# Linformer attention followed by a hard-swish feed-forward: when one load of q starts, and one weight load cut in two

## The chip, the cores and the metric

The kernel runs on one core of a Trainium2 chip. A core has TensorE (PE, the matrix engine), VectorE (DVE), ScalarE (ACT), GpSimd (POOL) and SyncE (SP), each with its own instruction queue that runs in order. Transfers between HBM and the on-chip memory are issued from such a queue and carried out by 16 DMA engines. In this kernel POOL issues all loads (the profile's queue q0, software_dynamic) and SP all stores, DMA transposes and re-layouts but a few (q1, hardware_dynamic). The metric is the device time of one execution in microseconds.

## The reference

```
def _attn_ref(q, k, v, E, F):                 # q, k, v: 8 batches, 8 heads, 1024 tokens, 64
    k_proj = einsum('ks,bhsd->bhkd', E, k)    # 1024 tokens projected to 64
    v_proj = einsum('ks,bhsd->bhkd', F, v)
    scores = matmul(q, k_proj^T) / sqrt(64)
    attn   = softmax(scores)                  # over the 64 projected keys
    return matmul(attn, v_proj)

x = attn_out as 8192 tokens x 512
h = x @ w_in                                  # 512 -> 2048
g = h * clip(h + 3, 0, 6) / 6
out = g @ w_out                               # 2048 -> 512, float32
```

## The kernel before

**Stages.** A batch has 1024 tokens, handled as two blocks of 512. For a block, the first product (`first_group`, one call for each of 16 groups of 128 columns of w_in) makes h in PSUM, 8 matmuls each; ACT and DVE turn it into g (`h_out`). The second product (`second_group`) multiplies g by w_out, in four parts of 128 tokens, each in four quarters over the 2048 columns. All matmuls are cut into two halves of 64 columns (`in_columns`, line 169).

**Attention of the next batches** is laid between these groups. `project` multiplies k and v by E and F, `turn` has SP transpose the projected keys (kT, line 212) and q (qT, line 157), `scores` (line 229) multiplies qT and kT, `exps` takes the exponential on ACT, `add_up` and `spread_sums` build the softmax sums on DVE, take reciprocals, write them to DRAM (`turned_rows`, line 287, two small transfers) and read them back spread over the partitions (`rec`, line 293, eight transfers: two for each of four pairs of heads `recs[0]` to `recs[3]`). `values` (line 250) multiplies the weights by the projected v, and `scaled` (line 262) multiplies that by the reciprocals into xT, the input of the first product of the next batch.

**Order.** The schedule is written by hand: the order in the program is the order on each engine. In the main loop `plan` maps (part of the second product, quarter) to a step of attention. While batch 1 is in its feed-forward (b = 1), batch 2 is projected, its sums end at (5, 2), its values for pairs 0 and 1 come at (6, 1), its products with the reciprocals at (6, 4), and pairs 2 and 3 at (7, 1). Then b = 2 starts with `TwoGroups(...).parts((0, 1, 2), (3,))`: the first two groups of w_in take pairs 0, 1 and 2 of xT (12 matmuls) and then pair 3. Within b = 2 batch 3 is projected at (0, 2) and its scores come at (1, 4). Batch 3's qT is not made in `turn`: a step at the end of b = 1 puts its two DMA transposes on SP's queue ahead of batch 3's kT.

**Loads.** At the start POOL issues, in this order: k and the first half of q of batch 0 in pairs of heads, v of batch 0, w_in in eight pieces (two of 128 columns, five of 256, the last of 512), the second half of batch 0's q, w_out in four quarters, and k, v, q of batch 1. POOL's loads go round eight semaphores, and a load waits until the load eight places before it has landed. Later batches are loaded by `turn`: POOL copies one element (`mark`) of the last DMA transpose, which makes it wait for that transpose, and then issues the three loads of the next batch. The order is k, v, q, but for batch 3, where it is q, k, v. The k, v and q tiles have two buffers each.

Of the kernel before, what the change touches and what calls it, by code (L numbers as in the profile page):

```python
# [9 lines left out]
bf16 = mybir.dt.bfloat16  # L10
# [5 lines left out]
def kernel(  # L16
# [11 lines left out]
    nc = tc.nc  # L28
# [27 lines left out]
    att = ctx.enter_context(tc.tile_pool(name="att", bufs=2))  # L56
# [36 lines left out]
    def raw_tile(name):  # L93
        return kqv_pool.tile([P, H, SO, D], bf16, tag=name, name=name)


    kqv = {0: {n: raw_tile(n) for n in ("k", "q", "v")}}
# [16 lines left out]
        load_pair("v", j)  # L114

    def load_kqv(b, order="qkv"):
        kqv[b] = {}
        for n in order:
            kqv[b][n] = raw_tile(n)
            nc.gpsimd.dma_start(out=kqv[b][n], in_=kqv_dram[n][b])  # L120
# [3 lines left out]
    def load_w_in(lo, n):  # L124
        nc.gpsimd.dma_start(out=w_in_sb[:, :, lo:lo + n], in_=w_in_v[:, :, lo:lo + n])

    for lo, n in ((0, 128), (128, 128), (256, 256), (512, 256), (768, 256),
                  (1024, 256), (1280, 256), (1536, 512)):
        load_w_in(lo, n)
    load_q0(1, slice(0, H))  # L130
    for i in range(SB):
        c = slice(i * FO // SB, (i + 1) * FO // SB)
        nc.gpsimd.dma_start(out=w_out_sb[:, c, :], in_=w_out_v[:, c, :])
    load_kqv(1, "kvq")


# [16 lines left out]
    def q_transposed(b):  # L153

        t = qT_pool.tile([P, KO, 2, TOK], bf16, tag="qT", name="qT")
        for i in range(2):
            nc.sync.dma_start_transpose(t[:, i * KO // 2:(i + 1) * KO // 2].rearrange("p j a (m n) -> p (j a m) n", n=P),
                                        kqv[b]["q"][:, i * H // 2:(i + 1) * H // 2].rearrange("p h s d -> p (h s d)"))
        return t
# [11 lines left out]
    def rec_tile():  # L171
        return att.tile([P, 2, TOK], f32, tag="rec", name="rec", bufs=4)
# [9 lines left out]

    later = []

    class Attention:
# [23 lines left out]
        def turn(self):  # L211
            nc.sync.dma_start_transpose(self.kT, self.kp.rearrange("p h a d -> p (h a d)"))
            last = self.kT[:1, 0, :1]
            if self.b != 3:
                qT_dma[self.b] = q_transposed(self.b)
                last = qT_dma[self.b][:1, 0, 0, :1]
            if self.b + 1 < B:
                mark = att.tile([1, 1], bf16, tag="mark", name="mark")
                nc.gpsimd.tensor_copy(mark, last)  # L219
                load_kqv(self.b + 1, "qkv" if self.b == 2 else "kvq")  # L220


        def scores(self, j, *allocs):
# [52 lines left out]
        def spread_sums(self):  # L276
            turned, other = [att.tile([P, KO * 32], f32, tag="turned", name="turned", bufs=2) for _ in range(2)]
            inv = att.tile([KP, KO * 32], f32, tag="inv", name="inv", bufs=1)
            nc.vector.transpose(turned, self.parts.rearrange("p j c -> p (j c)"))
            for t in range(NB):  # L280
                here, there = slice(t * KP, t * KP + 32), slice(t * KP + 32, (t + 1) * KP)
                nc.vector.tensor_copy(other[here], turned[there])
                nc.vector.tensor_add(inv[t * 32:(t + 1) * 32], turned[here], other[here])
            nc.vector.reciprocal(inv, inv)
            rows = dram.tile([NB, KO, 32, 32], f32, tag="turned_rows", name="turned_rows")
            for t in range(NB):
                nc.sync.dma_start(out=rows[t].rearrange("j c i -> c j i"),
                                  in_=inv[t * 32:(t + 1) * 32].rearrange("c (j i) -> c j i", j=KO))
            by_head = rows.rearrange("t j (a c) i -> j a t (c i)", a=2)
            self.recs = [rec_tile() for _ in range(KO)]  # L290
            for j in range(KO):
                for a in range(2):
                    nc.sync.dma_start(out=self.recs[j][a * D:(a + 1) * D],
                                      in_=by_head[j, a:a + 1].to_broadcast([D, NB, TOK]))

# [434 lines left out]
```

## Time and profile before

| | us |
|---|---|
| median of 4 runs | 502.46 |
| lowest and highest | 502.1 to 504.07 |
| the profiled execution | 502.1 |
| its span, first to last instruction | 500.3 |
| PE busy | 494.0 (99%) |
| DVE, ACT, POOL busy | 285.5, 239.7, 38.7 |
| software DMA queue (POOL's loads) | 29.36 MB, 37.6% of 16 engines' span |
| hardware DMA queue (SP's and ACT's) | 38.02 MB, 30.6% |

The DMA row of the page, in 40 slices of 12.5 us, shows where transfers crowd: the first eight slices are at nine tenths or nearly so, and later slices go up and down with the loads of each batch.

```profile
DMA  9999999897759799449950799309411261101112
```

A timeline row of the profile gives the start, the length, engine, line, operation, what it writes and reads, and in brackets how long the engine idled before it and what ended that. For a DMA the length is the time its issue holds the queue; a row of DMA issues ends with the size of each and the time from its issue to its landing. Sizes are those of the bf16 destination.

### The profile page before, as it was taken

Reading aid. Unit: us, or ns where it says so; the run is one execution under the profiler, and the core shown is the slowest. Engines: PE = TensorE matmul, PEld = TensorE weight load, DVE = VectorE, ACT = ScalarE, POOL = GpSimd, SP = SyncE. Lnnn points to the kernel's source line nnn. Section 1 sums busy time; section 2 is a strip of 40 time slices with the busy share of each in tenths; the row PEclk is TensorE's granted clock in tenths of the full one; section 3 lists DMA queues with packets and bytes.
Section 4 is the critical chain, followed back from the end, with each engine's and each line's share of the span. In section 5 each row is a group of like instructions: output and inputs, shape, how many; then the busy total and the mean of one; then the engine's idle time right before and its main releaser. Section 6 shows DMA issues by size and latency. Waiting matters only on the chain.

```text
span 500.3 us, 11177 instructions
## 1 busy us (share of the span) xinstructions
PE 494.0 (99%) x4802; PEld 256.2 (51%) x4802; DVE 285.5 (57%) x438; ACT 239.7 (48%) x414; POOL 38.7 (8%) x58
## 2 busy tenths in 40 slices
PE   8899999999999999999999999999999999999997
PEld 4454554555455555555555545555455555555554
DVE  3572836886659674666648654674755656334420
ACT  3656566665355345433563344643446344343431
POOL 8620020200020020002000020000000000000000
PEclk9999999999999999999999999999999999999999
DMA  9999999897759799449950799309411261101112
GB/s 166 197 204 208 187 173 233 151 213 174 178 94 222 173 198 216 104 118 226 213 111 22 182 190 222 75 25 232 115 43 44 60 176 45 43 22 43 44 43 84
DMA packets 83618, 68.43 MB, mean 137 GB/s; under 512 B 38256, under 2 KB 69232, under 8 KB 83568
## 3 DMA queue, kind: packets, MB, share of 16 engines
q0 software_dynamic: 32480, 29.36, 37.6%
q1 hardware_dynamic: 50864, 38.02, 30.6%
q8 instruction: 37, 0.61, 0.5%
q10 hardware_dynamic: 224, 0.33, 0.3%
q14 instruction: 13, 0.11, 0.1%
HBM read 71.83 MB, written 16.97 MB: 177 GB/s over the span
## 4 chain that ended last, share of the span: by engine, by line
PE 96%; DMA 2%; POOL 2%; issue 0%; ACT 0%; ACTq 0%; POOLq 0%
PE mm L169 89%; PE at L169 2%; DMA v<-in_v_dram 2%; PE mm L250 1%; PE at L229 1%; PE at L250 1%; PE mm L229 1%; POOL q L102 1%; POOL k L106 1%; POOL v L106 0%; PE at L425 0%; PE at L405 0%; PE at L391 0%; PE at L418 0%; POOL ident masks.py:199 0%
## 5 line engine op out<-in xcount | busy, mean ns | idle before, releaser
L514 DVE SCALAR_TENSOR_TENSOR g<-r,mm 128x512 bf16<-128x512 f32 x256 | 174.4, 687 | 143.1 <-ACT r L513 142.4
L169 PE MATMUL mm<-w_out_sb,g 128*64 128x512 bf16 (+2 forms) x2080 | 235.7, 376 | 0.0
L169 PE MATMUL mm<-xT,w_in_sb 128*64 128x512 bf16 x2048 | 231.1, 379 | 0.0
L513 ACT ACTIVATE r<-mm 128x512 f32<-128x512 f32 x256 | 152.7, 598 | 74.2 <-PE mm L169 73.2
L169 PEld LDWEIGHTS <-g 128*64 128x64 bf16 x2080 | 115.0, 110 | 106.5 <-issue 7.3
L169 PEld LDWEIGHTS <-w_in_sb 128*64 128x64 bf16 x2048 | 115.9, 110 | 104.7 <-issue 0.6
L548 ACT COPY o_sb<-mm 128x512 f32<-128x512 f32 x58 | 34.0, 586 | 150.0 <-PE mm L169 149.6
L270 DVE TRANSPOSE_TENSOR_REDUCE parts<-aT 128x32 f32<-128x1024 bf16 x24 | 28.8, 1227 | 0.0
L262 DVE TENSOR_TENSOR xT<-at,rec 128x512 bf16<-128x512 f32 x32 | 20.5, 683 | 8.7 <-ACT rec L181 5.8
L238 ACT ACTIVATE aT<-at 128x512 bf16<-128x512 f32 x38 | 20.7, 620 | 7.6 <-PE at L229 7.6
L262 DVE TENSOR_TENSOR xT<-mm,rec 128x512 bf16<-128x512 f32 x24 | 15.5, 686 | 7.3 <-PE mm L250 7.2
L219 POOL COPY mark<-qT 1x1 bf16<-1x1 bf16 x5 | 0.9, 178 | 202.0 <-DMA qT<-q 202.0
L205 DVE CAST kp<-at 64x512 bf16<-64x512 f32 x14 | 9.0, 678 | 11.2 <-PE at L169 11.2
L169 PE MATMUL at<-k,e_t 128*64 128x512 bf16 x56 | 13.2, 379 | 0.0
L169 PE MATMUL at<-v,f_t 128*64 128x512 bf16 x56 | 13.2, 379 | 0.0
L238 ACT ACTIVATE aT<-mm 128x512 bf16<-128x512 f32 x18 | 9.7, 603 | 7.1 <-PE mm L229 7.1
L208 DVE CAST vp<-at 64x512 bf16<-64x512 f32 x14 | 9.7, 694 | 0.4
L538 DVE COPY o_sb<-mm 128x384 f32<-128x384 f32 x1 | 0.6, 558 | 15.1 <-PE mm L169 15.1
L169 PEld LDWEIGHTS <-e_t 128*64 128x64 bf16 x56 | 6.2, 110 | 5.7
L89 PE MATMUL mm<-ones 128*128 128x512 bf16 x18 | 6.8, 504 | 1.5 <-DVE ones L82 1.5
L229 PEld LDWEIGHTS <-kT 64*64 64x64 bf16 x224 | 5.7, 106 | 4.4 <-issue 3.5
L503 DVE TENSOR_TENSOR xT<-at,rec 128x512 bf16<-128x512 f32 x4 | 2.5, 684 | 8.2 <-PE at L425 8.2
(68 smaller groups left out, 151.3 us busy)
## 6 DMA issues: line engine op xcount, KB each, us to landing
out_dram<-o_sb SPq DMA_DIRECT2D x63, 256.0 KB, 4.4
rec<-turned_rows SPq DMA_DIRECT2D x48, 256.0 KB, 6.7
k<-in_k_dram POOLq DMA_DIRECT2D x7, 1024.0 KB, 10.5
v<-in_v_dram POOLq DMA_DIRECT2D x7, 1024.0 KB, 15.6
q<-in_q_dram POOLq DMA_DIRECT2D x7, 1024.0 KB, 20.4
w_out_sb<-in_moe_w_out_dram POOLq DMA_DIRECT2D x4, 512.0 KB, 16.1
w_in_sb<-in_moe_w_in_dram POOLq DMA_DIRECT2D x5, 256.0 KB, 10.0
k<-in_k_dram POOLq DMA_DIRECT2D x4, 256.0 KB, 5.5
```

The costliest lines, as they stand in the source:

```text
L89: nc.tensor.matmul(ps, ones[:, :P], ones, start=True, stop=True)
L169: nc.tensor.matmul(ps[lo:lo + width], stationary[:, lo:lo + width], moving, **flags)
L205: nc.vector.tensor_copy(self.kp[:, :, a, :], self.ps[:KP].rearrange("p (h d) -> p h d", d=D))
L208: nc.vector.tensor_copy(self.vp[a * KP:(a + 1) * KP], self.ps[KP:].rearrange("p (h d) -> p h d", d=D))
L229: nc.tensor.matmul(tiles[r][t * KP:(t + 1) * KP, a * HT:(a + 1) * HT], self.kT[r * D:(r + 1) * D, 2 * j + a, :], qT[r * D:(r + 1) * D, j, ...
L238: when(lambda r=r: nc.scalar.activation(aT[:, :, r, :], tiles[r].rearrange("p (a n) -> p a n", a=2), AF.Exp, scale=scale))
L250: nc.tensor.matmul(tiles[t][c:c + D], stationary(r, 2 * j + a), self.weights(j, a)[r:r + KP], start=True, stop=True)
L262: when(lambda t=t: nc.vector.tensor_mul(self.xT[:, j, t, :], av[t], rec[:, t]))
L270: nc.vector.tensor_reduce(out=self.parts[:, j], op=ALU.add, axis=mybir.AxisListType.X, apply_transpose=True, in_=self.aT[j].rearrange("p a ...
L513: nc.scalar.activation(r, h_ps, AF.Relu, bias=0.5, scale=1.0 / 6.0)
L514: nc.vector.scalar_tensor_tensor(g[:, fo, :], r, 1.0, h_ps, op0=ALU.min, op1=ALU.mult)
L548: (copy or nc.scalar.copy)(o_sb, o_ps)
```

## The change

`load_kqv` may now be called more than once for a batch. The mark and the load behind it have become a function, `behind_that`. For batch 3 `turn` of batch 2 now loads only k and v behind batch 2's qT. The load of batch 3's q is issued at the end of `spread_sums` of batch 2, behind a copy of one element of `recs[1]`, the third of the eight transfers that bring the reciprocals back. On POOL the copy stands behind the two loads and ahead of the mark for batch 4. The last 512 columns of w_in come in two loads of 256. No engine but POOL has another instruction or another order.

```
-        kqv[b] = {}
+        kqv.setdefault(b, {})
...
     for lo, n in ((0, 128), (128, 128), (256, 256), (512, 256), (768, 256),
-                  (1024, 256), (1280, 256), (1536, 512)):
+                  (1024, 256), (1280, 256), (1536, 256), (1792, 256)):
         load_w_in(lo, n)
...
+    def behind_that(last, *what):
+        mark = att.tile([1, 1], bf16, tag="mark", name="mark")
+        nc.gpsimd.tensor_copy(mark, last)
+        load_kqv(*what)
...
             if self.b + 1 < B:
-                mark = att.tile([1, 1], bf16, tag="mark", name="mark")
-                nc.gpsimd.tensor_copy(mark, last)
-                load_kqv(self.b + 1, "qkv" if self.b == 2 else "kvq")
+                behind_that(last, self.b + 1, "kv" if self.b == 2 else "kvq")
...
                     nc.sync.dma_start(out=self.recs[j][a * D:(a + 1) * D],
                                       in_=by_head[j, a:a + 1].to_broadcast([D, NB, TOK]))
+            if self.b == 2:
+
+                behind_that(self.recs[1][:1, 0, :1], 3, "q")
```

## The prediction

> **What bounds the kernel now.** I read the page first, then PE by stretches, then the waits that PE itself has, and only then the transfers that the change touches. The page gives the span, PE's busy share and the chain that ended last:
>
> ```profile
> span 500.3 us, 11177 instructions
> PE 494.0 (99%) x4802; PEld 256.2 (51%) x4802; DVE 285.5 (57%) x438; ACT 239.7 (48%) x414; POOL 38.7 (8%) x58
> PE 96%; DMA 2%; POOL 2%; issue 0%; ACT 0%; ACTq 0%; POOLq 0%
> ```
>
> The last line is the chain by engine. Its 4% outside PE are the first 19.35 us, before the last load of batch 0's v has landed; after that it is PE alone. The stretches say the same: the busy column of PE equals the length of each stretch (us, PE, PEld, DVE, ACT, POOL, granted clock, DMA share, GB/s).
>
> ```profile
> 20.00:57.00 37.00, 37.00 (x376) 19.02 (x378) 21.14 (x32) 23.25 (x40) 6.84 (x9) 1.00 1.28 214
> 57.00:117.00 60.00, 60.00 (x610) 30.70 (x608) 41.06 (x63) 36.83 (x64) 5.62 (x8) 1.00 1.04 179
> 117.00:130.00 13.00, 13.00 (x124) 6.24 (x122) 9.58 (x16) 4.71 (x8) 0.00 (x0) 1.00 0.77 204
> 130.00:146.00 16.00, 16.00 (x150) 8.27 (x146) 8.15 (x13) 5.84 (x10) 2.54 (x4) 1.00 0.56 110
> ```
>
> So between 20 and 146 us, where all of the change lies, PE does not wait as far as this view can tell, at a granted clock of 1.00. A faster transfer has nothing to give there; a slower one can cost, once its consumer's slack is used up. The question is where slack is thin.
>
> **Part 1, the last quarter of w_in in two loads.** POOL's timeline and the DMA issues of single stretches give each landing as start plus us to landing.
>
> ```profile
> 17.26 0.74 POOL L125 DMA_DIRECT2D w_in_sb<-in_moe_w_in_dram  x1 [0.56 <-DMA v<-in_v_dram]
> 19.59 0.74 POOL L125 DMA_DIRECT2D w_in_sb<-in_moe_w_in_dram  x1 [1.58 <-DMA v<-in_v_dram]
> 20.32 0.89 POOL L102 DMA_DIRECT2D q<-in_q_dram  x1
> 21.20 0.77 POOL L133 DMA_DIRECT2D w_out_sb<-in_moe_w_out_dram  x1
> ```
> ```profile
> w_in_sb<-in_moe_w_in_dram POOLq DMA_DIRECT2D x1, 256.0 KB, 10.1
> w_in_sb<-in_moe_w_in_dram POOLq DMA_DIRECT2D x1, 512.0 KB, 10.3
> q<-in_q_dram POOLq DMA_DIRECT2D x1, 512.0 KB, 12.4
> w_out_sb<-in_moe_w_out_dram POOLq DMA_DIRECT2D x1, 512.0 KB, 14.1
> ```
>
> Landings: the 256 KB piece at 17.26 + 10.1 = 27.4, the last quarter at 19.59 + 10.3 = 29.9, q's second half at 32.7, the first quarter of w_out at 35.3. The stream is full, one transfer behind the other. PE's timeline shows who uses them:
>
> ```profile
> 33.42 0.61 PE L405 MATMUL at<-ident,q 128*64 128x128 bf16 x16
> 33.86 1.03 PE L169 MATMUL mm<-xT,w_in_sb 128*64 128x512 bf16 x8
> 34.73 0.61 PE L405 MATMUL at<-ident,q 128*64 128x128 bf16 x16
> 35.31 1.05 PE L169 MATMUL mm<-w_out_sb,g 128*64 128x512 bf16 x8
> ```
>
> A group of w_in takes 34.73 - 33.86 = 0.87 us, so the group that first needs the last quarter starts at 33.42 - 3 x 0.87 = 30.8, 0.9 after its landing: loading its first half sooner removes no wait, it widens a slack that is there. The transposes of q have 33.4 - 32.7 = 0.7. The product with w_out has none: the first run of 16 transposes is followed after 0.44 us, the second after 35.31 - 34.73 = 0.58, so PE waits some 0.14 us until w_out has landed at 35.3. Whatever lengthens the stream ahead of w_out is paid in full. The quarter took 29.9 - 27.4 = 2.5 us; a 256 KB piece takes 27.4 - 26.1 = 1.3 (the piece before it starts at 15.96 and also needs 10.1). Two pieces: 2.6, so **+0.1 us**; by the rows' rounding it is 0 to +0.2. POOL issues one load more, 0.74 us, and each later load waits for one landing more (at most eight of its loads are under way, by the semaphores): q's second half starts about 21.1, w_out about 22.1. Both still have over 10 us of queue in front, so their landings do not move by that. Batch 1's k, v and q move by the same 0.1, their projection with them.
>
> The Trainium skill, in "DMA: Bandwidth & Descriptors", section "Rules for kernel authors", speaks against the split: gather small transfers into large ones, as each carries a fixed cost, which its section on the anatomy of one DMA puts at about 2 us. By that rule the term would be about +2 us; the spacing of 1.3 us between pieces in a full queue contradicts it, since a fixed latency overlaps with the next transfer.
>
> **Part 2, q of batch 3 behind the reciprocals.** Before, POOL issues q, k, v of batch 3 together, at 95.70, 96.57 and 97.44; they land after 9.6, 13.8 and 18.8 us, at 105.3, 110.4 and 116.2. The small writes of the reciprocals (line 287) start at 113.25 in the tail of v and take 3.1 us; the page's median is 1.5. After, k and v take the first two places and end at about 110.4, so the small writes run alone and the eight broadcasts back start 1.2 us sooner, about 115.4 (bounds: no gain, and 3.1 - 1.5 = 1.6). DVE gets them sooner:
>
> ```profile
> 121.70 1.29 DVE L262 TENSOR_TENSOR xT<-at,rec 128x512 bf16<-128x512 f32 x2 [1.72 <-DMA rec<-turned_rows]
> 124.17 1.29 DVE L262 TENSOR_TENSOR xT<-at,rec 128x512 bf16<-128x512 f32 x2 [1.18 <-DMA rec<-turned_rows]
> 127.77 1.28 DVE L262 TENSOR_TENSOR xT<-mm,rec 128x512 bf16<-128x512 f32 x2
> 128.96 1.28 DVE L262 TENSOR_TENSOR xT<-at,rec 128x512 bf16<-128x512 f32 x2
> ```
>
> Those 1.72 and 1.18 us are DVE's and not PE's (PE is busy 13.00 of 13.00 around them). **Gain 0.**
>
> What it adds: POOL's one-element copy waits for the third broadcast, which landed at 117.97 + 4.9 = 122.9 and would land at 121.7. With 0.18 for the copy and 0.35 before the next issue, q starts at about 122.2. Alone it needs 9.6 (the row at 95.70): 131.8. But the other five broadcasts and the output stores fill the hardware queue until about 128, and a stretch with both queues at work shows how they share:
>
> ```profile
> q0 software_dynamic: 97, 0.10, 58.2%
> q1 hardware_dynamic: 91, 0.18, 53.7%
> ```
>
> That is 85 to 86 us; with the loads alone, 102 to 103 us, queue 0 moves 201 packets. So q runs at half speed for about 5 us, loses 2.5 and lands at **134.3** (bounds 131.8, and 136.8 if it gets nothing meanwhile). Who waits for it, in SP's timeline:
>
> ```profile
> 121.92 9.70 SPq L549 DMA_DIRECT2D out_dram<-o_sb  x3
> 131.80 4.88 SPq L157 DMA_TRANSPOSE qT<-q  x2
> 139.92 0.34 SPq L549 DMA_DIRECT2D out_dram<-o_sb  x1
> 140.36 1.22 SPq L212 DMA_TRANSPOSE kT<-kp  x1
> ```
>
> SP stands at q's transposes from 131.8. Behind them in its queue are a store and kT. Issued at 134.3 the transposes are through by 139.2, before the store's own 139.92, so kT keeps its 140.36. kT lands 2.6 us after issue, at 143.0, and PE first takes kT and qT at 146.10 (line 229): 3.1 us to spare, so PE suffers only if q lands after 139.92 - 4.88 + 3.1 = 138.1. Even the upper bound leaves 1.3. **Cost 0.** On POOL the next instruction behind the new wait is the copy for batch 4, which waits until 143.13 in any case.
>
> The other side of the sharing is the broadcasts. The last landed at 121.21 + 7.4 = 128.6; shifted by 1.2 it is 127.4, and sharing from about 124 on adds 1 to 3 us: 128.4 to 130.4. PE needs the product made from it in the fourth part of the next batch's first two groups, 12 matmuls of 0.108 us after 130.47, at 131.8; the product takes 0.7, so the landing may be as late as 131.1. **Cost 0, with 0.7 to 2.7 us to spare**, the thinnest cover of this part.
>
> **Sum.** +0.1 and 0. The profiled execution took 502.1 us (span 500.3 and 1.8 around it), so 502.2 by its own measure; the median of the four runs is 502.46, 0.36 above it, so I say **502.6 us**.
>
> **The rivals.**
> - *The broadcasts turn late (slower, 12%).* An output store that starts at 72.15, under the loads, lands after 6.0 us; the one at 131.29, without them, after 2.2. If the last broadcast pays that 3.8 on top of 127.4, it lands at 131.2 and PE loses 0.1; without the 1.2 us head start, 132.4 and 1.3. If all of q goes ahead of it, k to v spacing 110.4 - 105.3 = 5.1, it lands at 132.5 to 133.7 and PE loses 1.4 to 2.6. With +0.1 from part 1 that is 502.6 to 505.2, typically 504.4. It counts as slower from a landing after about 132.5. Against it: the two queues' even packet counts, and the broadcasts are queued before q starts.
> - *The runs not profiled do wait (faster, 6%).* The median exceeds the profiled run by 0.36 us and one run by 2.0. If late reciprocals or the late quarter of w_in cause that, the change takes it away. The median could fall by 0.36 to 502.1; for more than 0.3% (about 1.5 us, what a measurement of this kernel can tell from no change), the start-up must also shrink by some 1.1, say 500.8. Against it: w_out's landing stays behind the same bytes.
> - *The start-up pays a fixed cost (inside the forecast's bin, 7%).* If the split cost POOL's 0.74 us in the stream, 503.2.
>
> **How the numbers follow.** The forecast, with this last rival, has 82%: within 0.3%. Its own range is 501.9 to 503.4: down by 0.36 and a little noise, up by 0.74 and a little noise. For the range I let it reach part of the slower rival: 501.8 to 503.8.
>
> **What would show it.** In the changed profile PE's busy time equals the stretch from 117 to 146 us again; DVE's waits for reciprocals of 1.72 and 1.18 fall to about 0.5 each; q starts near 122 and lands near 134; SP's transposes start near 134, kT still near 140.4; the last product of batch 2 (128.96) stays below 131.1; w_out is first used near 35.4. I am wrong if PE shows idle time near 130 to 135 (broadcasts) or near 146 (kT), or a first product with w_out later than 36.

## The result, and the profile after

The changed kernel takes 501.97 us (median of 52 runs, 501.46 to 502.61) against 502.64 for the kernel before (79 runs, 501.62 to 505.93): a ratio of 0.9984, with a 95% interval from 0.9979 to 0.9988, so 0.6 to 1.1 us faster. Beside the median the spread went: 4.3 us between the kernel before's extremes, 1.2 after. The two medians lie within 0.3% of each other, and 501.97 lies inside the stated range, but the direction that was forecast, +0.1 us, is wrong.

The page of the changed kernel: span, PE's busy time, and the chain by engine.

```profile
span 500.6 us, 11181 instructions
PE 494.0 (99%) x4802; PEld 256.0 (51%) x4802; DVE 285.8 (57%) x438; ACT 239.7 (48%) x414; POOL 39.6 (8%) x60
PE 93%; DMA 4%; POOL 2%; SPq 0%; issue 0%; ACT 0%; ACTq 0%; POOLq 0%
```

Nothing here shows the gain; this span is even 0.3 us longer than the one of before. The profiled execution of the kernel before, 502.1 us, was one of its quicker ones, and the changed kernel's, 502.38, one of its slower ones, with a wait for batch 4's qT near 183 us that I return to. The transfers went as described. POOL's timeline of the changed kernel:

```profile
95.78 0.88 POOL L120 DMA_DIRECT2D k<-in_k_dram  x1 [0.35 <-PE mm L169]
96.65 0.88 POOL L120 DMA_DIRECT2D v<-in_v_dram  x1
121.54 0.18 POOL L187 CAST mark<-rec 1x1 bf16<-1x1 f32 x1 [24.01 <-DMA rec<-turned_rows]
122.05 0.88 POOL L120 DMA_DIRECT2D q<-in_q_dram  x1 [0.34 <-issue]
```

SP's timeline of it:

```profile
113.32 0.81 SPq L290 DMA_DIRECT2D turned_rows<-inv  x2
115.27 5.21 SPq L296 DMA_DIRECT2D rec<-turned_rows  x8
120.57 10.82 SPq L555 DMA_DIRECT2D out_dram<-o_sb  x3
133.77 4.72 SPq L157 DMA_TRANSPOSE qT<-q  x2
139.69 0.35 SPq L555 DMA_DIRECT2D out_dram<-o_sb  x1
140.14 1.22 SPq L217 DMA_TRANSPOSE kT<-kp  x1
```

Its DMA issues in two short stretches, the small writes at 113 us and q at 122 us (the last number is us to landing):

```profile
turned_rows<-inv SPq DMA_DIRECT2D x2, 16.0 KB, 1.5
q<-in_q_dram POOLq DMA_DIRECT2D x1, 1024.0 KB, 11.6
```

The small writes land after 1.5 us instead of 3.1, the broadcasts start at 115.27 instead of 116.64, q lands at 122.05 + 11.6 = 133.7, SP's transposes of q start at once, kT keeps its place. What the broadcasts' earlier landing is worth shows in PE's timeline around 126 us. The kernel before:

```profile
122.59 3.62 PE L169 MATMUL mm<-xT,w_in_sb 128*64 128x512 bf16 x32
126.11 1.05 PE L169 MATMUL mm<-w_out_sb,g 128*64 128x512 bf16 x8
127.09 0.61 PE L250 MATMUL mm<-aT,vp 64*64 64x512 bf16 x4
127.33 0.59 PE L250 MATMUL at<-aT,vp 64*64 64x512 bf16 x4
127.85 2.78 PE L169 MATMUL mm<-w_out_sb,g 128*64 128x512 bf16 x24
```

The same stretch of the changed kernel:

```profile
122.66 3.62 PE L169 MATMUL mm<-xT,w_in_sb 128*64 128x512 bf16 x32
126.11 1.03 PE L169 MATMUL mm<-w_out_sb,g 128*64 128x512 bf16 x8
127.07 0.41 PE L253 MATMUL mm<-aT,vp 64*64 64x512 bf16 x4
127.31 0.39 PE L253 MATMUL at<-aT,vp 64*64 64x512 bf16 x4
127.62 2.78 PE L169 MATMUL mm<-w_out_sb,g 128*64 128x512 bf16 x24
```

Compare starts, not busy times. From the four groups of w_in (first row) to the next product with w_out (second row) it is 126.11 - 122.59 = 3.52 us before and 3.45 after. From there to the last row it is 127.85 - 126.11 = 1.74 before and 1.51 after; of the eight value matmuls between, the first four took 0.61 and 0.41. PE lost 0.07 + 0.23 = 0.3 us here, which no idle time shows, since the modelled ends of pipelined matmuls cover it. DVE's timelines say why. The kernel before, behind the product at 124.17 that the prediction shows:

```profile
125.38 2.47 DVE L514 SCALAR_TENSOR_TENSOR g<-r,mm 128x512 bf16<-128x512 f32 x4
```

The changed kernel:

```profile
120.43 1.29 DVE L265 TENSOR_TENSOR xT<-at,rec 128x512 bf16<-128x512 f32 x2 [0.38 <-DMA rec<-turned_rows]
122.93 1.29 DVE L265 TENSOR_TENSOR xT<-at,rec 128x512 bf16<-128x512 f32 x2 [1.21 <-PE mm L169]
124.36 0.69 DVE L520 SCALAR_TENSOR_TENSOR g<-r,mm 128x512 bf16<-128x512 f32 x1
128.75 1.28 DVE L265 TENSOR_TENSOR xT<-at,rec 128x512 bf16<-128x512 f32 x2
```

In DVE's order, the products with the reciprocals of pairs 0 and 1 stand ahead of the g of the four groups of w_in, and PE's next product needs one of the PSUM banks that those g's free (PSUM is the memory that PE writes its results to; the pool `ps_mm` has four banks, one for each of the four groups). After, the first g ends at 124.36 + 0.69 = 125.05, a microsecond ahead of PE. Before, the products started at 124.17 and the first g at 125.38; it ended at 126.07, and PE started at 126.11. There was no slack at all: by these rows each us by which the second half of `recs[1]` lands after about 124.0 should delay PE by one. The experiments try this.

### The profile page after: what moved, and what is told of

Its sections match the earlier page's. It is cut to its first block, busy times and chain, and to the rows that moved or that the text cites. A ratio compares the mean times of both kernels' runs of the same rounds, so it can differ in the third digit from the quotient of the medians.

```text
span 500.6 us, 11181 instructions
## 1 busy us (share of the span) xinstructions
PE 494.0 (99%) x4802; PEld 256.0 (51%) x4802; DVE 285.8 (57%) x438; ACT 239.7 (48%) x414; POOL 39.6 (8%) x60
## 4 chain that ended last, share of the span: by engine, by line
PE 93%; DMA 4%; POOL 2%; SPq 0%; issue 0%; ACT 0%; ACTq 0%; POOLq 0%
PE mm L169 87%; PE at L169 2%; DMA v<-in_v_dram 2%; DMA qT<-q 2%; PE at L232 1%; PE mm L253 1%; PE at L253 1%; PE mm L232 1%; POOL q L102 1%; POOL k L106 1%; POOL v L106 0%; PE at L431 0%; SPq L217 0%; PE at L411 0%; PE at L397 0%
```

## The experiments

Theory A: the reciprocals of batch 2 land late by an amount that varies with the tail of batch 3's loads, and PE pays through the PSUM bank. Theory B: the start-up pays, where the last quarter of w_in is sometimes late. The kernels ran in three groups of four, each group on one chip and with the kernel before timed beside it: 503.29 us in the first (`win_only`, `q_only`, `order_only`, `rec_late1`), 503.38 in the second (`load_more`, `q_early`, `gate_last`, `early_next`), 503.17 in the third (the rest). Ratios are to that kernel before.

**Each part alone.** `win_only`:

```
-                  (1024, 256), (1280, 256), (1536, 512)):
+                  (1024, 256), (1280, 256), (1536, 256), (1792, 256)):
```

> Only the last quarter of w_in comes in two loads; q of batch 3 is loaded as before. Theory A (the reciprocals of batch 2 come late by a varying amount, PE waits a little for the PSUM banks that DVE frees late near 127 us): the time stays where the kernel before is, within 0.2 us of its median (+0.1 expected), with the same spread. Theory B (the start-up, where the last quarter of w_in is sometimes late): the time falls by 0.5 to 0.8 us and the spread shrinks as in the changed kernel.

Measured: 503.29 us, ratio 1.0006 (0.9994 to 1.0018). Its profile has the wait at PE's product after the four groups: 3.87 us where 3.45 would do. `q_only` is the whole change without that line.

> Only the load of q of batch 3 is moved behind the reciprocals; w_in as before. Theory A: faster than before by 0.6 to 0.9 us, with the changed kernel's small spread, and in the trace the second value matmul near 127.1 follows the first at once, where it took 0.2 us more before. Theory B: within 0.2 us of the kernel before, with its spread.

Measured: 501.90 us (7 runs, 501.54 to 502.47), ratio 0.9975 (0.9964 to 0.9985). The gain and the small spread belong to q; Theory B is out. The first four value matmuls take 0.41 us in its trace, as in the changed kernel.

**Order without the wait.** `order_only`:

```
-                load_kqv(self.b + 1, "qkv" if self.b == 2 else "kvq")
+                load_kqv(self.b + 1, "kvq")
```

> The kernel before with batch 3 loaded in the order k, v, q and no wait: the same bytes in the same stretch, so the loads still end near 116 us. Theory A in the form that the small writes of the reciprocals are held up by the tail of the loads: as the kernel before, within 0.3 us, and the small writes still take about 3 us. If instead the order matters (k and v early), the time falls by 0.5 us or more.

Measured: 503.52 us, ratio 1.0000 (0.9991 to 1.0010). The order of the three loads is worth nothing that this can tell. Its profiled execution, its longest (504.99 us), took a large wait, so the mechanism stands there in the open. DVE's timeline of it:

```profile
126.84 1.29 DVE L262 TENSOR_TENSOR xT<-at,rec 128x512 bf16<-128x512 f32 x2 [1.86 <-DMA rec<-turned_rows]
128.04 2.47 DVE L514 SCALAR_TENSOR_TENSOR g<-r,mm 128x512 bf16<-128x512 f32 x4
```

PE's timeline of it:

```profile
123.59 3.62 PE L169 MATMUL mm<-xT,w_in_sb 128*64 128x512 bf16 x32
128.78 1.05 PE L169 MATMUL mm<-w_out_sb,g 128*64 128x512 bf16 x8 [1.56 <-DVE g L514]
```

The waits of PE in it (who waited for whom; us in total, times, longest):

```profile
PE mm L169 <- DVE g L514: 1.6, 1, 1.6
```

The small writes took 4.0 us here; the products wait for the broadcast until 126.84, the first g starts at 128.04 and ends 0.69 later, at 128.73, and PE starts at 128.78, 5.19 us after its four groups where 3.45 would do: 1.7 us lost. Another 1.0 us this execution had lost in its start-up: its four groups start at 123.59 instead of 122.59, and the granted clock was 0.66 from 15 to 20 us, where the first profile has 1.00.

**The kernel before, looked at again** (`before_again`, the unchanged program, one execution).

> The kernel before once more, for a second profile of it. By Theory A its trace has a wait of PE for the PSUM bank near 126 us of between 0.1 and 2 us, equal to what the second pair's reciprocals land later than 124.0 us after allowing for the shift of the start-up.

Measured: 503.59 us, span 501.8. The small writes took 3.9 us. DVE's timeline of it:

```profile
125.42 1.29 DVE L262 TENSOR_TENSOR xT<-at,rec 128x512 bf16<-128x512 f32 x2 [0.90 <-DMA rec<-turned_rows]
126.62 2.47 DVE L514 SCALAR_TENSOR_TENSOR g<-r,mm 128x512 bf16<-128x512 f32 x4
```

PE's timeline of it:

```profile
122.89 3.62 PE L169 MATMUL mm<-xT,w_in_sb 128*64 128x512 bf16 x32
127.35 1.05 PE L169 MATMUL mm<-w_out_sb,g 128*64 128x512 bf16 x8 [0.84 <-DVE g L514]
```

The same site: 126.62 + 0.69 = 127.31, PE at 127.35, 4.46 us after the groups, so 1.0 lost where the first profile lost 0.07. Of the 1.5 us between the two spans, this is 0.9, and 0.3 is the start-up. In these profiles the kernel before varies mostly because this wait varies; the start-up varies too.

**A longer tail.** `load_more` adds to the kernel before a load of 256 KB that nobody reads:

```
                 load_kqv(self.b + 1, "qkv" if self.b == 2 else "kvq")
+                if self.b == 2:
+                    nc.gpsimd.dma_start(out=extra, in_=kqv_dram["q"][4][:, 0:2])
```

> The kernel before with one more load of 256 KB, which nobody reads, behind batch 3's q, k and v (about 1.3 us of the load queue). Theory A (each us by which the second pair's reciprocals land later costs PE one us, through the PSUM bank that DVE frees late): the small writes of the reciprocals land 1 to 1.3 us later and the time rises by 0.9 to 1.4 us over the kernel before. If the loads' tail does not matter to PE: within 0.3 us of the kernel before.

Measured: 504.24 us against 503.38, 0.86 more (ratio 1.0019, interval 1.0004 to 1.0035). The small writes took 4.6 us and PE waited 1.6 us at the same place. It agrees with Theory A, just under what was expected; the interval, 0.2 to 1.8 us, does not quite shut out the 0.3 us of the other reading.

**Late without any load.** `rec_late1` is the changed kernel with the small writes done twice for batch 2:

```
-            for t in range(NB):
-                nc.sync.dma_start(out=rows[t].rearrange("j c i -> c j i"),
...
+            for _ in range(2 if self.b == 2 else 1):
+                for t in range(NB):
+                    nc.sync.dma_start(out=rows[t].rearrange("j c i -> c j i"),
...
```

> The changed kernel, but batch 2's reciprocals are written to DRAM twice, the second pair of writes behind the first: the eight broadcasts start about 1.5 to 2 us later, without any load beside them. Theory A: PE waits again near 126 to 132 us and the time rises by 0.3 to 1.5 us over the changed kernel. If lateness of the reciprocals costs PE nothing, the time stays within 0.2 us of the changed kernel.

Measured: 505.29 us, 3.4 over `q_only` on the same chip (ratio to the kernel before 1.0041, interval 1.0019 to 1.0063). The direction is Theory A's; the size was missed, and the waits of PE in its profile, of one of its longest executions (507.17 us), tell why:

```profile
PE at L232 <- DMA qT<-q: 2.0, 1, 2.0
PE mm L169 <- DVE g L521: 1.0, 1, 1.0
```

The wait for the bank is 1.0, as expected. The other is new: q, and so batch 3's qT and kT, slid back, batch 4's loads with them, and those met batch 3's own small writes near 164 us (4.5 us to land), so batch 4's qT came 2.0 us late near 186. The chain of marks hands a delay from batch to batch. After that wait TensorE ran at a lower granted clock for a few us (0.62 from 186 to 189 us, 0.81 from 189 to 192), which cost this execution some more.

**All profiles of this place together.** Where the loads of batch 3 outlast the issue of the small writes, the broadcasts start 0.4 to 0.5 us after the last load has landed, in all five profiles: at 116.64 behind 116.2 in the first profile of the kernel before, 117.53 behind 117.1 in `win_only`, 117.79 behind 117.3 in `before_again`, 118.47 behind 118.0 in `order_only`, 118.51 behind 118.0 in `load_more`. And PE pays one for one, as the rows of the first profile said. Take its 0.07 us, add what the product of pair 1 starts later than 124.17, take off what the four groups start later than 122.59: that gives 0.43 us for `win_only`, 1.02 for `before_again`, 1.74 for `order_only`, 1.76 for `load_more`, and 1.15 for `rec_late1`, where no load is under way. From the groups to the next product PE lost 0.42, 1.01, 1.74, 1.75 and 1.15.

**Where else q could go.** `q_early` loads batch 3's q right behind batch 2's loads:

```
-                load_kqv(self.b + 1, "qkv" if self.b == 2 else "kvq")
+                load_kqv(self.b + 1, "kv" if self.b == 2 else "kvq")
+                if self.b == 1:
+                    load_kqv(3, "q")
```

> The kernel before, but batch 3's q is loaded right behind batch 2's k, v and q, near 70 us, with no wait for the reciprocals; k and v of batch 3 as before near 96 us. Theory A: only the emptied load queue near 113 us counts, so this is as fast as the changed kernel within 0.3 us (0.6 to 1.2 us under the kernel before) with its small spread. If the wait on the reciprocals itself is what helps, it stays with the kernel before.

Measured: 504.98 us, ratio 1.0031 (1.0014 to 1.0047). The expectation failed as to the time. At the small writes, now at 116.4 us, it did what was asked: they land in 1.5 us, and PE's next product follows its four groups after 3.46 us, as in the changed kernel. So the empty queue removes the wait, and the copy's wait on the reciprocals is not needed for it. But the fourth load now covers batch 2's own kT transpose, which takes 7.7 us to land instead of 2.6, and PE pays for late transposes near 102 us, as its waits show:

```profile
PE mm L231 <- DMA qT<-q: 2.1, 1, 2.1
```

`early_next` does the same, with w_in as before, and moves batch 4's q to the place behind batch 2's reciprocals.

> q of batch 3 early as in the run with q near 70 us, and q of batch 4 in the place behind batch 2's reciprocals, so that only k and v of batch 4 are loaded near 144 to 155 us and the small writes of batch 3's reciprocals near 163 us find the queue empty. If the wait of PE for batch 4's qT near 183 us (0.3 us in the changed kernel's profile) is a second case of the same collision, it goes: 0.1 to 0.4 us under the changed kernel. If not: within 0.15 us of it; slower if q's load disturbs SP's transposes of batch 3 near 134 us.

Measured: 505.68 us, ratio 1.0033 (1.0018 to 1.0049): the same wait, 2.0 us near 101, and after it a lower clock (last section). What the move of batch 4's q is worth can't be read from it.

`gate_last` is `q_only` with the copy taken from the last of the eight broadcasts:

```
+                behind_that(self.recs[3][D:D + 1, 0, :1], 3, "q")
```

> The change of q alone, but behind the last of the eight broadcasts instead of the third: q starts about 5 us later, near 127, and lands near 137 to 138. By the slack that was worked out (PE suffers from q landing after 138) the time is within 0.4 us of the changed kernel; if the slack on that side is smaller, as a later q also shifts batch 4's loads and its transposes near 183 us, it rises by 0.5 to 2 us.

Measured: 504.79 us, ratio 1.0025 (1.0014 to 1.0036), 2.9 over `q_only` by the medians of the two chips. PE's timeline of it:

```profile
147.48 0.41 PE L232 MATMUL mm<-qT,kT 64*64 64x256 bf16 x8 [1.46 <-DMA kT<-kp]
```

q lands at 127.77 + 10.2 = 138.0, and this already costs 1.5 us at kT and, by the shift of batch 4's loads, another 1.2 at qT near 186. SP's transposes start at 138.16; the store behind them, with 4.2 us to land instead of 2.2, and kT at 143.70 with 3.7 us instead of 2.7, do the rest.

`gate_first` is the changed kernel with the copy from the first broadcast (`self.recs[0]`).

> The changed kernel, with q of batch 3 behind the first of the eight broadcasts instead of the third: q starts about 2 us sooner, near 120, and takes more of the broadcasts' rate. If sharing with the load delays the second pair's reciprocals, PE's wait near 126 us comes back: 0.3 to 1 us over the changed kernel. If the broadcasts already queued keep their pace: within 0.2 us of it.

Measured: 501.89 us, ratio 0.9975 (0.9961 to 0.9989), beside 501.96 for the changed kernel on the same chip. The broadcasts already queued keep enough of their pace: `recs[1]` lands at 122.8 us, where the changed kernel has 122.6 to 122.8, so the wait does not come back.

**The wait near 183 us.** The changed kernel once more as yardstick (`after_again`), and `next_by_qT`:

```
+            elif self.b == 3:
+                last = qT_dma[3][:1, KO // 2, 0, :1]
```

> The changed kernel once more, as the yardstick for the next two on the same chip: 0.6 to 1.4 us under the kernel before.

> The changed kernel, with batch 4's loads behind the second half of batch 3's qT (landing near 140.5 us) instead of behind its kT (near 142.8). They end 2 us sooner, so the small writes of batch 3's reciprocals near 163 us meet less of them. If the wait of PE for qT near 183 us is the same collision: that wait goes, and the median falls by 0.05 to 0.3 us under the changed kernel. If the loads' start disturbs kT instead, PE waits near 146 us and it is slower by 0.5 us or more.

Measured: 501.96 us (0.9975, interval 0.9963 to 0.9987) and 502.04 us (0.9971, interval 0.9954 to 0.9987). Batch 4's loads start 1.5 us sooner, and batch 3's small writes take 1.5 us instead of 2.3 in `after_again` and 3.3 in the changed kernel's first profile, the one with the wait. Neither of the two new profiles has a wait near 183, and the medians agree, so nothing is gained that these runs can tell. No version was found that beats the changed kernel; `q_only` and `gate_first` equal it.

## Why the prediction was wrong

**The step that failed** is the line on DVE's waits: "Those 1.72 and 1.18 us are DVE's and not PE's (PE is busy 13.00 of 13.00 around them). **Gain 0.**" DVE's waits were a link of a chain that ends at PE. The profile held it, in two rows of PE and DVE side by side: the end of the first g, 126.07, against PE's next start, 126.11. I took a busy share of 100% for the absence of a wait, although PE's busy time is modelled and hides waits of a few tenths. And I took one execution for all: it lost 0.3 us there, another look at the same program 1.0 and more. What the term should have been is the typical loss. `q_only` measures it as 0.25% of 503.3 us, 1.3 us on that chip (0.15% to 0.36%); the result above has 0.6 to 1.1 for the whole change. The changed kernel takes 501.9 to 502.0 in every group; it is the kernel before that differs, 502.64 to 503.38, and why was not looked into.

**The rival had it.** "The runs not profiled do wait" named late reciprocals and the gap between the median and the profiled run. It was held down to 0.36 us because only four runs were known, and its larger size was sought in the start-up. Among the first four times, one stood 2.0 us above the profiled one, which was as good a hint.

**Part 1, +0.1 us.** The pieces did as worked out: the one ahead lands at 27.0, the two new ones at 28.3 and 29.7, 2.7 us instead of 2.5. But the 0.2 us did not reach PE. The first quarter of w_out lands at 35.3 in both profiles, and after, PE goes from the second run of transposes (34.95) to w_out (35.40) in 0.45 us, the distance it needs without a wait; only before was it 0.58. That w_out is first used near 35.4, as said, was luck: PE's transposes start 0.2 us later in that profile (33.64 against 33.42). `win_only` (1.0006 with 0.0012 either way) can't tell +0.1 from 0, and rules out both a gain of the size seen and a loss of 2 us.

**Part 2, the transfers.** These held: broadcasts 1.4 us sooner (1.2 worked out, bound 1.6), q's issue at 122.05 (122.2), its landing at 133.7 (134.3), SP's transposes at 133.77, kT at 140.14, the last product of batch 2 at 128.75, below 131.1. The wait of DVE at pair 0 fell to 0.38, below the 0.5 that was said. The one at pair 1 did not fall: 1.21 us, which the profile puts down to PE, and 0.91 in `after_again`, where the broadcast ended it. That row now starts 1.24 us sooner and so leaves DVE time enough; how long DVE waits there tells nothing of PE. The rival that the broadcasts turn late did not come true, not even in `gate_first`, which starts q before all eight are issued.

**The slack behind q** was worked out too generously. PE was to suffer only from a landing after 138.1; `gate_last` lands at 138.0 and costs 1.5 us at once and 1.2 later. Left out were that the store and kT can take 1 to 2 us longer to land when they follow the transposes closely, as they did here, and that any delay of kT is handed on to batch 4's loads. The place of the copy, the third broadcast, is not critical towards the front but is towards the back.

## What to carry to other kernels

When an engine off the critical path waits for a transfer, follow what stands behind that wait in its own queue down to the buffers that the critical engine needs next, and compare the two times; a busy share of 100% does not answer it, as the 0.3 us hidden here show. If several runs of one program spread by more than the effect in question, a single profile may miss the wait: look at a second one, and at the slowest run. And judge a load not by its own consumer alone, but by which short transfers meet its tail.

## What the runs showed of the hardware

Two small writes of 16 KB took 1.5 us to land alone, and 3.1 to 4.6 us when issued while the last megabyte of a load from another queue was still coming in; what waited for them then started 0.4 to 0.5 us after that load had landed. A kT transpose went from 2.6 to 7.7 us under a load (`q_early`).

A wait of PE can cost more than its length. After the wait of 2.0 us in `early_next` the granted clock fell to half, and the 24 matmuls behind the scores took 4.4 us (101.84 to 106.24), where `q_early` took 2.7 (102.98 to 105.69). The columns are those of the stretches in the prediction; the clock is the third number from the end.

```profile
95.00:100.00 5.00, 4.08 (x38) 1.93 (x34) 4.22 (x8) 3.38 (x6) 1.03 (x2) 1.00 1.23 202
100.00:103.00 3.00, 1.94 (x34) 1.22 (x36) 0.43 (x1) 1.08 (x2) 0.90 (x2) 0.92 0.85 75
103.00:106.00 3.00, 3.00 (x18) 1.20 (x14) 1.16 (x2) 2.19 (x5) 0.00 (x0) 0.51 1.20 196
```

`rec_late1` shows the same after 2.0 us:

```profile
186.00:189.00 3.00, 2.37 (x18) 1.00 (x19) 0.89 (x2) 1.08 (x2) 1.96 (x4) 0.62 0.83 221
```

`q_early` kept 1.00 after 2.1 us, and after the waits of 1.6 us in `order_only` and `load_more` it stayed at 1.00 too. The Trainium skill ("TensorE: Matmul & The Clock Gate", section "HAM oscillation — how this bites in real kernels") warns of idle gaps longer than about 3.4 us; in these runs a lower clock followed waits of 2.0 to 2.1 us in two of three cases.
